# Attention and two MoE layers in one kernel: scores of two units in one TensorE visit, k and q in one load, three of sixteen quadrant copies issued by GpSimd

## The chip, the cores and the metric

The kernel runs on one core of a Trainium2 chip. The time is device microseconds from start to end of one execution. Before the change, three runs gave 1076.23, 1076.69 and 1080.57 us (median 1076.69).

## What is computed

Attention over 4 batches x 8 heads, 576 positions, head size 64, where scores under (row maximum - tau) are dropped. Its result, 2304 tokens x 512, goes through two MLP layers ("MoE" in the names) of 512 -> 2048 -> 512, the first with ELU, the second with a leaky ReLU. All is float32.

```
scores = (1/8) * q @ k^T
scores = where(scores >= max(scores) - tau, scores, -1e9)
x = softmax(scores) @ v                       # -> 2304 x 512
h = x @ w_in;   g = where(h > 0, h, exp(min(h, 0)) - 1);   x = g @ w_out
h = x @ w2_in;  g = maximum(0.01 * h, h);                  out = g @ w2_out
```

## The kernel before

**Attention.** Two heads form a pair; a *unit* is 64 query rows of a pair (128 rows on 128 partitions), 9 units for each of 16 pairs, 144 in all. A *group* is one pair with units 0 to 3 or 4 to 8, so 32 groups of 4 or 5 units (function `group`). For a group SyncE loads k, q and v (L425, L426, L428). For each unit (`unit`): four float32 matmuls of 64x64 by 64x288 make the scores s in PSUM, each in its own quarter of the array (`qk`, L445); VectorE scales them into ss in SBUF with the row minimum (L449) and makes thr from it (L454); ScalarE applies the threshold and the exponent with row sums (L457, L460) into e; VectorE takes the reciprocal of the sum (L463); GpSimd normalises e (L464); VectorE transposes e in blocks of 32x32 into the group's tile t (L472). When all units of a group are there, 16 copies of a quadrant of t into p by DMA (32 partitions each, 80 or 100 KB, L500) put the blocks in their places; then ten float32 matmuls multiply p with v (L514), and the result goes into x (L313 or L314). The first four groups go through TensorE transposes (L481) and need no copies. Buffers: two each of k, q, v, p and t, two of s in PSUM, three of ss and of e.

**MoE.** Every MoE matmul is split into three passes of float32r (a rounded high part and a rest, xh/xl, wih/wil, gh/gl). `step_h` makes h (L552), then g with gh and gl; `step_y` adds to y (L595). Seven blocks of 256 tokens of the first layer's first half (eight of sixteen slices of the hidden size) run beside the attention; all other MoE work comes after it, with 512 tokens a block. Weights are loaded as 64-bit words (wraw, L321) and turned into a high and a low part on ScalarE, VectorE and GpSimd (`weight`).

**What sets the order.** Nothing is put in order by hand. Each operation is entered with a cost, a due time vt and the engines that may do it (`op`); `Order.run` then plays the program through once at build time, and on each engine takes next, of what its plan holds to be ready, the one that is due first. The engines then run that fixed order. Constants in `KN` shift the due times and name the engines that may do a kind of work (A, D, P for ScalarE, VectorE, GpSimd); SWITCH is the planned cost when TensorE goes between float32r and float32 work.

Of the kernel before, what the change touches and what calls it, by code (L numbers as in the profile page):

```python
# [31 lines left out]
UM = 5  # L32
WT = 32 * UM
BESIDE = 7
GP = 1
AHEAD = 2
PT = ()
NA = 0
ACTI = 150
# [8 lines left out]
    pad=18, stay=455.902, late=1.3, margin=0, look=0.00334927, warm=3, tu=2231.35, lead=19463, wv0=558.362,  # L48
    wv1=105.738, early=3916.94, boff=24778.1, bdt=5036.21, yoff=2387.88, coff=7772.05, wb=1110.19, w2a=4797.07,
    o1=-2440.15, o2=2533.02, o3=4472.77, o4=-3359.29, o5=5750.16, o6=-25.7749, mo=-550.861, ka='PA', kl='AD',  # L50
    kh='PAD', ko='D', kt='D', kx='AD', kxl='DP', km='DP', kg='A', kgl='P', kgl1='D', kd='P', kc='AD', kn='P', kv='A')

# [176 lines left out]
SWITCH = 170  # L229
LAND = 2100.0  # L230
ISSUE = 400
# [25 lines left out]
def attn_moe_kernel(ctx, tc, qT, kT, vn, tau, w1i, w1o, w2i, w2o, yp, out):  # L257
# [108 lines left out]
    k_r = ring(ap_, 2, [128, 2, HALF], F32, "k")  # L366
    q_r = ring(ap_, 2, [128, 128 * UM], F32, "q")
# [4 lines left out]
    ss_r = Ring(None, 3)  # L372
    es_ = [ac.tile([128, SX], F32, name=f"e{j}") for j in range(3)]
    for t in es_:
        nc.gpsimd.memset(t[:, S:SX], 0.0)
    e_r = Ring(itertools.cycle(es_).__next__, 3)
    ident = ac.tile([128, 128], F32, name="ident")
    make_identity(nc, ident)
    sm_r = {t: ring(ap_, 4, [128, 1], F32, t) for t in ("nm", "thr", "su")}
# [5 lines left out]
    sts = [ac.tile([128, S + 2], F32, name=f"ss{j}") for j in range(3)]  # L385
# [25 lines left out]
    slots, unit_no = [], itertools.count()  # L411

    def s_of(i):
        while len(slots) <= i and len(slots) < NP * NU:
            slots.append(s_r.new())
        return slots[i] if i < len(slots) else None


    def group(gi, p, vts):
# [4 lines left out]
        k, q, v = k_r.new(), q_r.new(), v_r.new()  # L424
# [11 lines left out]
        def unit(j, vt):  # L436
            un = next(unit_no)
            s, ss, e = s_of(un), ss_r.new(), e_r.new()
            nm, thr, su = (sm_r[t].new() for t in ("nm", "thr", "su"))

            def qk():
                for h in range(2):
                    for i in range(2):
                        r = slice(64 * i, 64 * i + 64)
                        nc.tensor.matmul(s()[64 * h:64 * h + 64, i, 0:HALF], q()[r, 64 * (n * h + j):64 * (n * h + j) + 64],  # L445
                                         k()[r, h], start=True, stop=True)

            o = op((PE, mm32(HALF), qk, True), ld, [k, q, s], vt)
            o = op((DVE, dve(S) + 160, lambda: nc.vector.tensor_scalar(  # L449
                out=ss()[:, 0:S].rearrange("p (j c) -> p j c", j=2), in0=s()[:, :, 0:HALF], scalar1=scl,  # L450
                scalar2=3.0e38, op0=ALU.mult, op1=ALU.min, accum_out=nm())), [o, tau_op], [s, ss, nm], vt + KN["o1"])
            ot = op(pick(KN["kt"], P=(245, lambda: nc.gpsimd.tensor_scalar(
                             out=thr(), in0=nm(), scalar1=taup, scalar2=1.0, op0=ALU.add, op1=ALU.mult)),
                         D=(150, lambda: nc.vector.tensor_scalar(  # L454
                             out=thr(), in0=nm(), scalar1=taup, scalar2=None, op0=ALU.add))),
                [o, tau_op], [nm, thr], vt + KN["o1"])
            o = op((ACT, act(S) + 95, lambda: nc.scalar.activation(  # L457
                out=ss()[:, 0:S], in_=ss()[:, 0:S], func=AF.Prelu, bias=thr(), scale=-1.0, alpha=STEEP)),
                [ot], [ss, thr], vt + KN["o2"])
            o = op((ACT, act(S) + 190, lambda: nc.scalar.activation(  # L460
                out=e()[:, 0:S + 1], in_=ss()[:, 0:S + 1], func=AF.Exp, bias=taun, accum_out=su())),
                [o], [ss, e, su], vt + KN["o2"])
            o = op((DVE, 150, lambda: nc.vector.reciprocal(out=su(), in_=su())), [o], [su], vt + KN["o2"])  # L463
            o = op(pick(KN["kn"], P=(pool_ts(S) + 90, lambda: nc.gpsimd.tensor_scalar(  # L464
                            out=e()[:, 0:S], in0=e()[:, 0:S], scalar1=su(), scalar2=1.0, op0=ALU.mult, op1=ALU.mult)),
                        D=(dve2(S), lambda: nc.vector.tensor_scalar(
                            out=e()[:, 0:S], in0=e()[:, 0:S], scalar1=su(), scalar2=None, op0=ALU.mult), PORT)),
                   [o], [su, e], vt + KN["o3"])
            cols = slice(32 * j, 32 * j + 32)

            if not by_pe:
                turned.append(op((DVE, dve(SX) + 70, lambda: nc.vector.transpose(  # L472
                    out=blocks(tg).rearrange("p d c q -> p c d q")[:, :, :, cols],
                    in_=e().rearrange("p (c d i) -> p c d i", d=4, i=32))), [o], [e, tg], vt + KN["o3"]))
                return
            s_of(un + AHEAD)
            t = (ya if gi < GP else s_r).new()

            def tr():
                for c in range(5):  # L480
                    nc.tensor.transpose(t()[:, c // 4, c % 4 * 128:c % 4 * 128 + 128], e()[:, c * 128:(c + 1) * 128], ident)  # L481

            o = op((PE, 5 * 109, tr, True), [o], [e, t], vt + KN["o3"])
            for z, m in ((0, 4), (1, 1)):
                turned.append(op(copy_of(KN["kc"], 128 * m, lambda z=z, m=m: blocks(pg)[:, :, 4 * z:4 * z + m, cols],
                                         lambda z=z, m=m: t()[:, z, 0:128 * m].rearrange(
                                             "p (c a i) -> p a c i", c=m, a=4)), [o], [t, pg], vt + KN["o3"] + 500))

        for j in range(n):
            unit(j, vts[j])  # L490
        vt = vts[n - 1] + KN["o3"]
        got = turned
        if not by_pe:
            got = []
            for z, (a, d) in enumerate((a, d) for d in range(4) for a in range(4)):
# [6 lines left out]
                if z * NA // 16 != (z + 1) * NA // 16:  # L502
# [165 lines left out]
    TU, u, ends = KN["tu"], 0, []  # L668
# [112 lines left out]
```

## Time and profile before

| | us |
|---|---|
| median of three runs | 1076.69 |
| the profiled execution's own time | 1082.72 |
| its span, first to last instruction | 1080.7 |
| TensorE busy | 1028.9 (95%) |
| VectorE busy | 605.8 (56%) |
| ScalarE busy | 501.4 (46%) |
| GpSimd busy | 225.8 (21%) |
| mean granted clock of TensorE | 0.987 |

The profile comes from one execution. Busy time of an engine leaves out the issuing of DMAs and waits on semaphores. Shares of the whole span mix two stages: attention beside the first MoE blocks (to about 440 us), where all engines work, and MoE alone after it, where the others have little to do.

### The profile page before, as it was taken

To read this page: it belongs to the slowest core of one execution; us is meant where nothing else is said; L and a number is where in the kernel's file an instruction comes from. 1 tells how busy PE (TensorE), PEld (TensorE's weight loads), DVE (VectorE), ACT (ScalarE), POOL (GpSimd) and SP (SyncE) were. 2 spreads that over 40 slices of the span, in tenths; PEclk is the share of its full clock that TensorE was granted. 3 is DMA by queue.
4 is the path that set the end of the run, shared out by engine and by line. 5 is a ranking of instruction groups with operands and counts; after the bars stand their busy time and mean duration, and the time that the engine had idled before them with its cause. 6 is when DMAs were issued, how large, how long until landed. Compare 5 with 4: busy or idle time off the path is not lost.

```text
span 1080.7 us, 17082 instructions
## 1 busy us (share of the span) xinstructions
PE 1028.9 (95%) x6294; PEld 802.5 (74%) x6294; DVE 605.8 (56%) x1374; ACT 501.4 (46%) x1017; POOL 225.8 (21%) x317
## 2 busy tenths in 40 slices
PE   7768999999999999899999999999999999999998
PEld 3435666656766667688888889888888888888898
DVE  6887867766767675799998438961311311221221
ACT  6977867756776674354554223531222222222221
POOL 4766635444544453000000000000000000000000
PEclk9969999999999999999999999999999999999999
DMA  5678666776776677436454012420100100010010
GB/s 191 194 171 223 186 177 190 201 201 172 205 209 195 177 190 188 136 117 195 125 152 153 1 39 69 127 79 0 39 1 1 38 2 1 1 39 1 1 39 21
DMA packets 54514, 120.14 MB, mean 111 GB/s; under 512 B 10400, under 2 KB 15008, under 8 KB 54432
## 3 DMA queue, kind: packets, MB, share of 16 engines
q1 hardware_dynamic: 54432, 119.05, 38.8%
q8 instruction: 50, 0.82, 0.3%
q14 instruction: 32, 0.26, 0.1%
HBM read 67.63 MB, written 9.44 MB: 71 GB/s over the span
## 4 chain that ended last, share of the span: by engine, by line
PE 81%; SPq 6%; DMA 5%; DVE 4%; ACT 2%; issue 2%; POOL 0%; DVEq 0%; ACTq 0%
PE y L595 34%; PE h L552 20%; PE hb L552 14%; PE v L514 6%; SPq L500 6%; PE s L445 5%; DMA q<-in_qT_dram 2%; DMA p<-t 1%; DMA v<-in_vn_dram 1%; DVE ss L449 1%; ACT e L460 1%; DMA wraw<-in_w1o_dram 1%; ACT ss L457 1%; DVE g L571 1%; PE v L394 0%
## 5 line engine op out<-in xcount | busy, mean ns | idle before, releaser
L595 PE MATMUL y<-gh,woh 128*128 128x512 f32 (+1 forms) x736 | 256.0, 348 | 0.8 <-DVE ysx L314 0.8
L595 PE MATMUL y<-gl,woh 128*128 128x512 f32 (+1 forms) x736 | 252.0, 342 | 0.0
L595 PE MATMUL y<-gh,wol 128*128 128x512 f32 (+1 forms) x736 | 252.0, 342 | 0.0
L302 DVE TENSOR_TENSOR gl<-g,gh 128x512 fp32r<-128x512 f32 (+1 forms) x128 | 82.3, 643 | 269.2 <-ACT g L578 261.4
L552 PE MATMUL h<-xh,wih 128*128 128x256 f32 (+1 forms) x480 | 168.0, 350 | 14.6 <-DVE g L571 9.8
L595 PEld LDWEIGHTS y<-gh,woh 128*128 128x128 f32 x736 | 138.7, 188 | 33.1 <-issue 11.0
L552 PE MATMUL h<-xl,wih 128*128 128x256 f32 (+1 forms) x480 | 159.1, 331 | 1.3 <-POOL xl L303 1.0
L552 PE MATMUL h<-xh,wil 128*128 128x256 f32 (+1 forms) x480 | 158.3, 330 | 0.0
L595 PEld LDWEIGHTS y<-gl,woh 128*128 128x128 f32 x736 | 138.9, 189 | 16.1
L595 PEld LDWEIGHTS y<-gh,wol 128*128 128x128 f32 x736 | 138.5, 188 | 16.3
L552 PEld LDWEIGHTS h<-xh,wih 128*128 128x128 f32 x480 | 91.0, 190 | 57.3 <-issue 16.1
L449 DVE TENSOR_SCALAR_CACHE_REDUCE ss<-s,scl 128x576 f32<-128x576 f32 x144 | 116.3, 808 | 22.7 <-PE s L445 21.8
L460 ACT ACTIVATE e<-ss,taun 128x577 f32<-128x577 f32 x144 | 111.3, 773 | 32.2 <-DVE t L472 27.7
L464 POOL TENSOR_SCALAR e<-e,su 128x576 f32<-128x576 f32 x144 | 108.0, 756 | 80.6 <-DVE su L463 73.4
L472 DVE STREAM_TRANSPOSE t<-e 128x640 f32<-128x640 f32 x128 | 103.8, 831 | 32.2 <-DMA p<-t 21.7
L457 ACT ACTIVATE ss<-ss,thr 128x576 f32<-128x576 f32 x144 | 108.8, 767 | 17.0 <-DVE thr L454 16.5
L445 PE MATMUL s<-k,q 64*64 64x288 f32 x1152 | 99.6, 436 | 12.6 <-DVE ss L449 9.7
L514 PE MATMUL v<-p,v 128*64 128x320 f32 (+1 forms) x640 | 95.5, 422 | 12.8 <-DMA p<-t 7.2
L552 PEld LDWEIGHTS h<-xl,wih 128*128 128x128 f32 x480 | 91.6, 191 | 11.0 <-POOL xl L303 1.8
L552 PEld LDWEIGHTS h<-xh,wil 128*128 128x128 f32 x480 | 91.3, 190 | 8.0
L552 PE MATMUL hb<-xl,wih 128*128 128x512 f32 (+1 forms) x256 | 94.5, 369 | 0.0
L552 PE MATMUL hb<-xh,wih 128*128 128x512 f32 (+1 forms) x256 | 94.5, 369 | 0.0
(436 smaller groups left out, 1180.7 us busy)
## 6 DMA issues: line engine op xcount, KB each, us to landing
p<-t SPq DMA_DIRECT2D x256, 100.0 KB, 3.2
p<-t SPq DMA_DIRECT2D x192, 80.0 KB, 2.3
v<-in_vn_dram SPq DMA_DIRECT2D x32, 320.0 KB, 3.7
k<-in_kT_dram SPq DMA_DIRECT2D x32, 288.0 KB, 3.1
wraw<-in_w1i_dram SPq DMA_DIRECT2D x16, 512.0 KB, 3.6
wraw<-in_w1o_dram SPq DMA_DIRECT2D x16, 512.0 KB, 3.8
wraw<-in_w2i_dram SPq DMA_DIRECT2D x16, 512.0 KB, 3.5
wraw<-in_w2o_dram SPq DMA_DIRECT2D x16, 512.0 KB, 3.5
```

The source lines that it names most:

```text
L302: return pick(who, D=(dve(n), lambda: nc.vector.tensor_tensor(**args()), PORT), P=(pool_tt(n), lambda: nc.gpsimd.tensor_tensor(**args())))
L445: nc.tensor.matmul(s()[64 * h:64 * h + 64, i, 0:HALF], q()[r, 64 * (n * h + j):64 * (n * h + j) + 64], k()[r, h], start=True, stop=True)
L449: o = op((DVE, dve(S) + 160, lambda: nc.vector.tensor_scalar(out=ss()[:, 0:S].rearrange("p (j c) -> p j c", j=2), in0=s()[:, :, 0:HALF], s ...
L457: o = op((ACT, act(S) + 95, lambda: nc.scalar.activation(out=ss()[:, 0:S], in_=ss()[:, 0:S], func=AF.Prelu, bias=thr(), scale=-1.0, alpha= ...
L460: o = op((ACT, act(S) + 190, lambda: nc.scalar.activation(out=e()[:, 0:S + 1], in_=ss()[:, 0:S + 1], func=AF.Exp, bias=taun, accum_out=su())),
L464: o = op(pick(KN["kn"], P=(pool_ts(S) + 90, lambda: nc.gpsimd.tensor_scalar(out=e()[:, 0:S], in0=e()[:, 0:S], scalar1=su(), scalar2=1.0, o ...
L472: turned.append(op((DVE, dve(SX) + 70, lambda: nc.vector.transpose(out=blocks(tg).rearrange("p d c q -> p c d q")[:, :, :, cols], in_=e(). ...
L500: q.dma_start(out=to[0]()[to[1], to[2]], in_=fr[0]()[fr[1], fr[2]])
L514: nc.tensor.matmul(ps()[64 * h:64 * h + 64, 0:64 * n], v()[:, h, c, :], blocks(pg)[:, 2 * h:2 * h + 2, c], start=(c == 0), stop=(c == 4))
L552: nc.tensor.matmul(hp(), w_()[:, cs], x_()[:, 0:tb], start=(k == 0 and z == 0), stop=(k == KC - 1 and z == 2))
L571: o = op((DVE, dve(tb), lambda: nc.vector.scalar_tensor_tensor(out=g()[:, cs], in0=g()[:, cs], scalar=0.0, in1=hp(), op0=ALU.min, op1=ALU. ...
L595: nc.tensor.matmul(ysl(yg, m), w_()[:, cs], g_()[:, 0:tb], start=(first and z == 0 and share == 0), stop=(last and z == 2 and end))
```

## The change

Scores of two units are made in one TensorE operation (`units` in place of `unit`; the fifth unit of a group stays alone), with one thr and one reciprocal for both, and with four buffers of ss and e. k, q and v lie in one DRAM tensor by group; k and q come in one load of 128 partitions. The call that enters a group's copies and its value product (`values`) is made after the next group's `group`. Of the sixteen quadrant copies of a group the sixth, eleventh and sixteenth are issued by GpSimd, and the copies go round the diagonals. Costs in the planner and its constants are set anew, and with them the engines that may take some of the small operations.

```diff
-AHEAD = 2
-NA = 0
-ACTI = 150
+NG = 3
+POOLI = 1000
-SWITCH = 170
+SWITCH = 91
...
-        ld = [op(sp(128, 2304, lambda: nc.sync.dma_start(out=k(), in_=kT[hp])), [], [k], due),
-              op(sp(128, 512 * n, lambda: nc.sync.dma_start(
-                  out=q()[:, 0:128 * n], in_=qT[hp][:, 128 * u0:128 * u1])), [], [q], due)]
-        lv = op(sp(128, 2560, lambda: nc.sync.dma_start(out=v(), in_=vn[hp])), [], [v], due + 8e3)
+        kq, v = in_r.new(), v_r.new()
+        cut = 2 * HALF + 128 * n
+        ld = [op(sp(128, 4 * cut, lambda: nc.sync.dma_start(
+            out=kq()[:, 0:cut], in_=kqv[gi * NE + p][:, 0:cut])), [], [kq], due)]
+        lv = op(sp(128, 2560, lambda: nc.sync.dma_start(
+            out=v().rearrange("p h c d -> p (h c d)"), in_=kqv[gi * NE + p][:, KQV - 10 * D:KQV])), [], [v], due + 8e3)
...
-        def unit(j, vt):
-            s, ss, e = s_of(un), ss_r.new(), e_r.new()
+        def units(js, vt):
+            m = len(js)
+            s, ss, e = ([r.new() for _ in js] for r in (s_r, ss_r, e_r))
...
+                for z, j in enumerate(js):
+                    for h in range(2):
+                        for i in range(2):
...
-            o = op((PE, mm32(HALF), qk, True), ld, [k, q, s], vt)
+            oq = op((PE, m * (mm32(HALF) + 150), qk, True), ld, [kq, *s], vt)
...
+            orc = op((DVE, 150, lambda: nc.vector.reciprocal(out=su()[:, 0:m], in_=su()[:, 0:m])), oe, [su],
+                     vt + KN["o2"])
...
-        for j in range(n):
-            unit(j, vts[j])
-        vt = vts[n - 1] + KN["o3"]
+        for j in range(0, n, 2):
+            units(range(j, min(j + 2, n)), vts[j])
+        return lambda: values(gi, p, n, w, vts[n - 1] + KN["o3"], by_pe, turned, tg, pg, v, lv, blocks)
...
-            for z, (a, d) in enumerate((a, d) for d in range(4) for a in range(4)):
+            for z, (a, d) in enumerate((a, (a + r) % 4) for r in range(4) for a in range(4)):
...
-                if z * NA // 16 != (z + 1) * NA // 16:
-                    got.append(op((ACT, ACTI, lambda copy=copy: copy(nc.scalar)), turned, [pg, tg], vt + KN["o4"],
+                if z * NG // 16 != (z + 1) * NG // 16:
+                    got.append(op((POOL, POOLI, lambda copy=copy: copy(nc.gpsimd)), turned, [pg, tg], vt + KN["o4"],
                                   lat=2500))
...
-            group(gi, p, [(u + j) * TU for j in range(u1 - u0)])
+            later = group(gi, p, [(u + j) * TU for j in range(u1 - u0)])
             u += u1 - u0
+            if held is not None:
+                held()
+            held = later
+            if gi < GP or p in PT or u == NP * NU:
+                held()
+                held = None
```

Three places of the resulting order. First TensorE in the middle of the attention, before (s are score matmuls, four for a unit; h and y are MoE):

```order
L445 MATMUL s<-k,q 64x288 x4
L595 MATMUL y<-gh,woh_1310 128x256
L595 MATMUL y<-gl,woh_1310 128x256
L595 MATMUL y<-gh,wol_1321 128x256
L552 MATMUL h<-xh_2302,wih_190 128x256
L552 MATMUL h<-xl_2319,wih_190 128x256
L552 MATMUL h<-xh_2302,wil_209 128x256
L552 MATMUL h<-xh_2135,wih_340 128x256
L552 MATMUL h<-xl_2145,wih_340 128x256
L552 MATMUL h<-xh_2135,wil_360 128x256
L445 MATMUL s<-k,q 64x288 x4
```

and after, at a like place:

```order
L446 MATMUL s<-in 64x288 x8
L591 MATMUL h<-xh_2035,wih_290 128x256
L591 MATMUL h<-xl_2047,wih_290 128x256
L591 MATMUL h<-xh_2035,wil_294 128x256
L591 MATMUL h<-xh_2041,wih_290 128x256
L591 MATMUL h<-xl_2057,wih_290 128x256
L591 MATMUL h<-xh_2041,wil_294 128x256
L591 MATMUL h<-xh_2049,wih_290 128x256
L591 MATMUL h<-xl_2061,wih_290 128x256
L591 MATMUL h<-xh_2049,wil_294 128x256
L553 MATMUL v<-p,v 64x320 x10
L446 MATMUL s<-in 64x288 x8
```

Score matmuls of one unit (x4) between MoE matmuls became those of two units (x8). Counted over the whole order, TensorE's stretches of float32 work (scores, transposes, value products) between MoE matmuls are 101 before and 67 after. Of the stretches of scores alone, 55 hold one unit and 13 hold two before; 4 and 30 after.

Second SyncE over one group and the start of the next, before (p<-t are the quadrant copies):

```order
L425 DMA k<-in_kT_dram 128x576
L426 DMA q<-in_qT_dram 128x640
L500 DMA p<-t_87 32x800 x7
L428 DMA v<-in_vn_dram 128x640
L500 DMA p<-t_87 32x800 x9
```

and after:

```order
L417 DMA in<-in_kqv_dram 128x1216
L539 DMA p<-t_87 32x800 x5
L419 DMA v<-in_kqv_dram 128x640
L539 DMA p<-t_87 32x800 x8
```

Nineteen issues for a group became fifteen, thirteen of them copies.

Third GpSimd, where the other three copies stand (e is a unit's normalisation, g, gh and gl are of the MoE chain), after:

```order
L469 TENSOR_SCALAR e_91<-e_91,su 128x576
L607 TENSOR_SCALAR g<-g 128x256
L469 TENSOR_SCALAR e_92<-e_92,su 128x576
L306 TENSOR_SCALAR gh<-g 128x256
L303 TENSOR_TENSOR gl<-g,gh 128x256 x2
L539 DMA p<-t_88 32x800 x3
L469 TENSOR_SCALAR e_89<-e_89,su 128x576
L469 TENSOR_SCALAR e_90<-e_90,su 128x576
```

The three stand between the normalisation of the group's last unit and those of later units. In all there are 84 of them; before there were none.

## Rows read from the trace of the kernel before

**Rows 1.** Busy time by stage: us, busy us of each engine (instructions), granted clock, DMA share, GB/s

```profile
0.00:100.00 100.00, 74.59 (x562) 40.78 (x564) 78.44 (x213) 78.60 (x161) 62.00 (x81) 0.89 0.70 198
100.00:440.00 340.00, 318.25 (x2663) 224.18 (x2659) 229.81 (x639) 224.71 (x495) 153.17 (x225) 0.99 0.71 190
440.00:1081.00 641.00, 636.05 (x3072) 537.49 (x3072) 297.56 (x524) 198.14 (x363) 10.61 (x12) 1.00 0.18 56
```

**Rows 2.** TensorE's waits, 100 to 440 us; last row 0 to 100 us: total, times, longest

```profile
PE h L552 <- DVE g L571: 9.4, 17, 0.6
PE v L514 <- DMA p<-t: 3.4, 6, 1.4
PE s L445 <- DMA q<-in_qT_dram: 2.4, 4, 0.9
PE v L514 <- issue: 1.7, 2, 1.2
PE v L514 <- DMA k<-in_kT_dram: 1.2, 1, 1.2
...
PE v L514 <- DMA p<-t: 3.9, 2, 2.4
```

**Rows 3.** Timeline of SyncE's queue: start us, us, instruction

```profile
232.28 5.18 SPq L500 DMA_DIRECT2D p<-t  x8
237.57 0.51 SPq L428 DMA_DIRECT2D v<-in_vn_dram  x1
238.13 4.96 SPq L500 DMA_DIRECT2D p<-t  x8
243.19 0.53 SPq L425 DMA_DIRECT2D k<-in_kT_dram  x1
243.76 0.44 SPq L426 DMA_DIRECT2D q<-in_qT_dram  x1
244.30 5.29 SPq L500 DMA_DIRECT2D p<-t  x7
```

**Rows 4.** Quadrant copies on SyncE, line L500: issue in ns, first and last start

```profile
L500 SPq DMA_DIRECT2D p<-t x448: 507/589/2061, 67.4 to 434.2; - x150
```

**Rows 5.** Waits of VectorE and ScalarE, 100 to 440 us

```profile
DVE t L472 <- DMA p<-t: 19.6, 13, 3.9
...
ACT e L460 <- DVE t L472: 26.8, 17, 3.7
```

**Rows 6.** Timeline of TensorE: a visit of one unit, and one of two

```profile
118.29 1.20 PE L445 MATMUL s<-k,q 64*64 64x288 f32 x16
119.42 0.39 PE L552 MATMUL h<-xh,wih 128*128 128x256 f32 x1
...
211.02 0.28 PE L552 MATMUL h<-xl,wih 128*128 128x256 f32 x1
211.14 0.28 PE L552 MATMUL h<-xh,wil 128*128 128x256 f32 x1
211.35 0.71 PE L445 MATMUL s<-k,q 64*64 64x288 f32 x8
212.00 0.39 PE L595 MATMUL y<-gh,woh 128*128 128x256 f32 x1
212.22 0.28 PE L595 MATMUL y<-gl,woh 128*128 128x256 f32 x1
```

**Rows 7.** Line L338 of VectorE, two instructions: ns min/median/max, start

```profile
L338 DVE SCALAR_TENSOR_TENSOR wb__751<-wa__718,wb__751 x1: 650/650/650, 58.2 to 58.2; 128x512 uint32<-128x512 uint32 x1
...
L338 DVE SCALAR_TENSOR_TENSOR wb__883<-wa__847,wb__883 x1: 1155/1155/1155, 71.4 to 71.4; 128x512 uint32<-128x512 uint32 x1
```

**Rows 8.** Timelines of TensorE and VectorE: group 17's scores, last transpose, value product

```profile
225.86 1.20 PE L445 MATMUL s<-k,q 64*64 64x288 f32 x16
...
238.52 0.84 DVE L472 STREAM_TRANSPOSE t<-e 128x640 f32<-128x640 f32 x1
...
258.74 1.08 PE L514 MATMUL v<-p,v 128*64 128x256 f32 x8
```

More of the change, by code (lines that the diff above doesn't have):

```diff
@@ L384, in attn_moe_kernel @@
     scl = ac.tile([128, 1], F32, name="scl")
[L385 removed]
+    sts = [ac.tile([128, S + 2], F32, name=f"ss{j}") for j in range(4)]
     ss_r.make = itertools.cycle(sts).__next__
@@ L457, in unit @@
[L457 to L463, printed above, removed]
@@ L476, in unit @@
[L476 to L487, printed above, removed]
@@ L489, in group @@
-        for j in range(n):
-            unit(j, vts[j])
-        vt = vts[n - 1] + KN["o3"]
+                             out=thr()[:, 0:m], in0=nm()[:, 0:m], scalar1=taup, scalar2=None, op0=ALU.add))),
+                [*om, tau_op], [nm, thr], vt + KN["o1"])
+            oe = []
+            for z in range(m):
+                o = op((ACT, act(S) + 95, lambda z=z: nc.scalar.activation(
+                    out=ss[z]()[:, 0:S], in_=ss[z]()[:, 0:S], func=AF.Prelu, bias=thr()[:, z:z + 1], scale=-1.0,
+                    alpha=STEEP)), [ot], [ss[z], thr], vt + KN["o2"])
+                oe.append(op((ACT, act(S) + 190, lambda z=z: nc.scalar.activation(
+                    out=e[z]()[:, 0:S + 1], in_=ss[z]()[:, 0:S + 1], func=AF.Exp, bias=taun,
+                    accum_out=su()[:, z:z + 1])), [o], [ss[z], e[z], su], vt + KN["o2"]))
@@ new lines, in copies, with turn @@
+            def copies(src, t, ot, c0, c1, z):
+                cols = slice(32 * js[z], 32 * js[z] + 32)
+                nn = 128 * (c1 - c0)
+                turned.append(op(copy_of(KN["kc"], nn, lambda: blocks(pg)[:, :, c0:c1, cols],
+                                         lambda: src().rearrange("p (c a i) -> p a c i", a=4, i=32)),
+                                 [ot], [t, pg], vt + KN["o3"] + 500))
+            def turn(dst, c, z):
+                nc.tensor.transpose(dst, e[z]()[:, c * 128:(c + 1) * 128], ident)
@@ new lines, in units, with tr @@
+            if not by_pe:
+                for z, j in enumerate(js):
+                    cols = slice(32 * j, 32 * j + 32)
+                    turned.append(op((DVE, dve(SX) + 70, lambda z=z, cols=cols: nc.vector.transpose(
+                        out=blocks(tg).rearrange("p d c q -> p c d q")[:, :, :, cols],
+                        in_=e[z]().rearrange("p (c d i) -> p c d i", d=4, i=32))), [on[z]], [e[z], tg], vt + KN["o3"]))
+            elif gi < GP:
+                for z in range(m):
+                    t = ya.new()
+                    def tr(t=t, z=z):
+                        for c in range(5):
+                            turn(t()[:, c // 4, c % 4 * 128:c % 4 * 128 + 128], c, z)
+                    o = op((PE, 5 * 109, tr, True), [on[z]], [e[z], t], vt + KN["o3"])
+                    copies(lambda t=t: t()[:, 0], t, o, 0, 4, z)
+                    copies(lambda t=t: t()[:, 1, 0:128], t, o, 4, 5, z)
+            else:
+                for z in range(m):
+                    t = v_ps.new()
+                    def tr(t=t, z=z):
+                        for c in range(4):
+                            turn(t()[:, c * 128:c * 128 + 128], c, z)
+                    o = op((PE, 4 * 109, tr, True), [on[z]], [e[z], t], vt + KN["o3"])
+                    copies(lambda t=t: t(), t, o, 0, 4, z)
+                t = v_ps.new()
+                def tr(t=t):
+                    for z in range(m):
+                        turn(t()[:, z * 128:z * 128 + 128], 4, z)
+                o = op((PE, m * 109, tr, True), on, [*e, t], vt + KN["o3"])
+                cols = slice(32 * js[0], 32 * js[0] + 32 * m)
+                turned.append(op(copy_of(KN["kc"], 128 * m, lambda: blocks(pg)[:, :, 4, cols].rearrange("p a (z i) -> p a z i", i=32),
+                                         lambda t=t: t()[:, 0:128 * m].rearrange("p (z a i) -> p a z i", a=4, i=32)),
+                                 [o], [t, pg], vt + KN["o3"] + 500))
```

99 lines of the change are left out of this document (48 added, 51 removed).

## The prediction

> **What bounds the kernel now.** I read the busy time by stage first [rows 1]. From 440 us on TensorE is busy for 636.05 of 641 us: that stage can give back at most 5 us, whatever is done. From 100 to 440 us, where attention runs beside the first MoE blocks, it is busy for 318.25 of 340 us, so 21.75 us are idle; in the first 100 us 25.4 us are idle. All that the change touches lies ahead of 440 us, and what it saves there moves the rest of the program forward, since TensorE is the engine that the last stage waits for.
>
> Second, TensorE's waits [rows 2]: from 100 to 440 us it waits 9.4 us for VectorE's g of the MoE chain, 3.4 us for quadrant copies (p<-t) ahead of a value product, 1.7 us for "issue" there, 2.4 and 1.2 us for loads of q and k. In the first 100 us another 3.9 us go to quadrant copies. No single wait is long; the question is whether one thing lies behind them.
>
> Third, SyncE's queue [rows 3]. One cycle from the copies at 232.28 to those at 244.30 is 12.0 us, and each issue begins about 0.1 us after the end of the one before: 16 copies, one v, one k, one q, and nothing idle. In all, 448 copies go out from 67.4 to 434.2 us [rows 4], 28 groups at 13.1 us. The 16 DMA engines are busy for 71% of that stage [rows 1], so it is issuing, not moving, that fills the cycle. SyncE's queue paces the groups, and TensorE with 94% busy runs just beside it. The queue's lateness shows elsewhere: VectorE's transposes wait 19.6 us in 13 places for copies to free the t buffer, and ScalarE waits 26.8 us for those transposes [rows 5]. VectorE's lateness is what TensorE sees as "g".
>
> Fourth, what a visit costs [rows 6]. MoE matmuls start 0.12 us apart. A visit of one unit takes 211.14 to 212.22 = 1.08 us between MoE starts where two spacings alone would be 0.24, so 0.84 us. Two units in one visit take 119.42 - 118.29 = 1.13 us against 212.00 - 211.35 = 0.65 us for one, so the second unit adds 0.48. Two apart cost 1.68 us, two together 1.32: **0.36 us are the visit's own**.
>
> **The change part by part.**
>
> *Two units in a visit.* By the order of the instructions TensorE goes from MoE matmuls to attention 101 times before and 67 times after (before, the planner already put some units together). 34 x 0.36 = **12.2 us** less on TensorE's own path. Nothing hides this: the engine is 94% busy there. The pair needs both score buffers free at once, but its first matmul waits only for the first of them, so I add no wait. VectorE's thr and reciprocal are made once for two units; VectorE is busy 229.81 of 340 us [rows 1], so I count that as nothing beyond what follows.
>
> *k and q in one load, three copies on GpSimd.* On SyncE a group falls from 16 to 13 copies, and from three loads to two. With (5.18 + 4.96)/16 = 0.63 us for a copy and 0.5 for a load [rows 3], 12.0 becomes 12.0 - 1.9 - 0.5 = 9.6 us: the queue is then idle for a fifth of the time and no longer paces. What is late next is TensorE itself. I take back the waits that this queue made: copies 3.4 + 1.7 + 3.9 = 9.0, loads 2.4 + 1.2 = 3.6, and of the 9.4 for g one half, 4.7, since half of the wait on VectorE may be its own work [rows 2]. Together **17.3 us**. Bounds: nothing, if the waits form again in another place, and the whole 21.75 + 3.9 us.
>
> *GpSimd's issues.* 84 copies go to its queue, behind the group's last normalisation, and the next units' normalisations and gl stand behind them. The trace of before has no issue by GpSimd. The nearest row is SyncE's copy, 0.507 to 2.061 us [rows 4]. GpSimd is busy 153.17 of 340 us [rows 1], 45% or 5.9 us of a group's 13.1. Three issues of 0.51 to 2.06 us make it 7.4 to 12.1 us; I take the short end, since the same kind of transfer is nearest, and add **2 us** for gl that comes later. Bounds: nothing, and the case "GpSimd paces" below.
>
> One instruction of VectorE with two inputs from SBUF (L338) took 650 ns at 58.2 us and 1155 ns at 71.4 us [rows 7], so something can hold it; the rows do not say what. The Trainium skill (SBUF — State Buffer, "Who interferes with whom" and "SBUF: two separate sides") says that the two share a pair of ports under an exclusive lock, and that a DMA issued by GpSimd starves while VectorE holds it, a 620 ns transfer taking some 3100 ns. That speaks against this change; the rows fit a conflict of the two, but no run here shows it for a DMA. By the same page a VectorE instruction with one SBUF input outside its two-port modes does not take the lock. If it held for each issue the group would stand at 5.9 + 3 x 3.1 = 15.2 us on GpSimd (an estimate from that page), and the program 28 x 2.1 = 59 us longer than now; by the row's price the sum keeps its 2 us.
>
> *"Values a group later".* The order of TensorE does not show this. Counted over the 23 groups from the eighth to the thirtieth, a group's value product stands behind 10.3 later units of scores before, and behind 8.2 after: **nearer**, by about two units, not farther. Deferring the call only changes the order in which the planner hears of it. So slack for the copies shrinks; this is the first rival.
>
> *Planner's numbers, the new layout, four buffers for e and ss.* They move work between ScalarE, VectorE and GpSimd (GpSimd takes weights' low words and some gh, VectorE some xl). All of these have idle time (VectorE 68%, ScalarE 66%, GpSimd 45% busy in the middle stage [rows 1]). I cost them at nothing; without that cover each microsecond would count fully. Behind 440 us TensorE is full, so nothing there either.
>
> Sum: -12.2 - 17.3 + 2 = **-27.5 us**. Against the profiled execution: span 1080.7 to 1053.2, its own time 1082.72 to 1055.2. The median of the runs lies 6.0 us below that time, 1076.69, so I predict 1076.7 - 27.5 = **1049 us**.
>
> **The rivals.**
>
> *Values wait again.* Group 17 as an example [rows 8, 3]: its last scores end at 227.0, its last transpose at 239.4, its copies start at 244.3, the product at 258.7: 31.7 us. Of these, 10.3 units at 13.1/4.5 us are 30.0. After the change a group takes 13.1 - 27.5/28 = 12.1 us, so 8.2 units are 22.0, and with the same 1.7 us of rest 23.7 us stand ahead of the product. Needed are 12.4 to the transpose, 14.4 - 3 x 0.63 = 12.5 from the first copy to the product, and one more unit's pass because two go together (VectorE's transpose 0.84 and, much the same, its read of the scores), 26.6 us. The forecast holds if the 12.4 shrink by 2.9, about what one wait on VectorE and one on ScalarE take (1.5 us and 1.6 us a time [rows 5]) and what SyncE no longer causes. If they shrink by half of that, a group takes 12.1 x 25.1/23.7 = 12.8 us, 28 x 0.3 = 8 us less than now, and with the first stage's 3.9 us 12 are won: **1065 us**. If by nothing, 13.6 us, and the program would stand at 1087. For it: the count of the order. Against it: SyncE is no longer the queue that holds the buffers.
>
> *GpSimd paces: slower.* Its group is 5.9 + 3c for an issue of c; beyond c = (13.1 - 5.9)/3 = 2.4 us it exceeds today's 13.1 us a group. An issue as long as the longest on SyncE, 2.06, that half the time waits out an L338 of 1.155 is 2.64 us: 13.8 us, +0.7 x 28 groups = +20, **1097 us**. For it: normalisations and gl have no other engine. Against it: L338 turns weights, in the first stage and after 440 us, and most copies go out between.
>
> *Everything goes.* If no wait of the middle stage is left (21.75), with the copies of the first stage (3.9) and the visits (12.2), it is -38 us: **1039 us**. For it: the queue lies behind most of them. Against it: g's chain has three engines of its own.
>
> *It does nothing*, because TensorE's clock or a new wait takes the visits' gain: 1077.
>
> **How the numbers follow.** Forecast 0.55, everything goes 0.14, values wait 0.19, GpSimd paces 0.09, nothing 0.03. The range 1033 to 1072 holds the first two and most of the third, and leaves out the slower case, "nothing" and the tails. A measurement of this kernel tells about 0.5%, 5.4 us, from no change: below 1071.3 is faster, above 1082.1 slower. Faster is 0.55 + 0.14 + 0.12 of "values wait" = 0.81; same is 0.05 more of that case and "nothing", 0.08; slower its last 0.02 and GpSimd's 0.09, 0.11.
>
> **What would show it.** Right: value products that start without idle time, SyncE's queue with gaps between groups, transposes' wait on copies nearly gone, the last quadrant copy near 407 us in place of 434.2 [rows 4], one group every 12.1 us. Right for the visits: s matmuls in runs of two units, MoE to attention 67 times. Wrong: p<-t ahead of the value products at 1 us or more in most groups (values wait), GpSimd over 90% busy from 100 to 410 us or normalisations that wait behind DMA issues (GpSimd paces), or a granted clock well below 0.97 in the middle stage.

## The result and the profile after

The changed kernel takes **1066.64 us** (median of four runs, 1065.84 to 1070.21) where the kernel before took 1076.46 beside it: a ratio of 0.9895, 95% interval 0.9873 to 0.9917, so 11.3 us faster by the ratio (9.8 by the two medians), less than half of the 27.5 forecast. One execution of a run below (a_fill) took 2567 us and is left out of its ratio. The profiled execution has a span of 1068.4 us (own time 1070.21), 12.3 less than before.

Busy time by stage (us; TensorE, its weight loads, VectorE, ScalarE, GpSimd; granted clock, DMA share, GB/s), to be held against [rows 1]:

```profile
0.00:100.00 100.00, 77.10 (x558) 43.42 (x559) 77.95 (x184) 77.73 (x162) 50.57 (x69) 0.81 0.60 187
100.00:440.00 340.00, 317.42 (x2713) 235.31 (x2712) 244.16 (x575) 227.06 (x497) 194.82 (x315) 0.98 0.73 198
440.00:1069.00 629.00, 624.81 (x3027) 529.00 (x3026) 273.96 (x470) 203.39 (x371) 19.03 (x28) 1.00 0.17 54
```

TensorE's idle time from 100 to 440 us is 22.6 us, as good as the 21.75 of before. Its waits there, to be held against [rows 2]:

```profile
PE h L591 <- ACT g L603: 4.2, 9, 0.5
PE s L446 <- DMA in<-in_kqv_dram: 4.2, 3, 2.0
PE v L553 <- DMA p<-t: 3.8, 3, 3.2
PE h L591 <- DVE g L610: 3.7, 6, 0.9
PE s L446 <- DVE ss L450: 2.7, 1, 2.7
```

The wait on VectorE's g fell from 9.4 to 3.7, but one on ScalarE's g, one for the load `in` and one for ss stand in its place; copies ahead of a value product are 3.8, in three places, where they were 3.4.

The quadrant copies (issue in ns min/median/max, first and last start), against [rows 4]; then waits of VectorE and ScalarE, against [rows 5]; then waits of SyncE's queue from 100 to 430 us:

```profile
L539 SPq DMA_DIRECT2D p<-t x364: 507/590/2264, 69.2 to 420.2; - x182
...
L539 POOL DMA_DIRECT2D p<-t x84: 496/498/685, 69.4 to 413.5; - x84
```

```profile
DVE t L489 <- DMA p<-t: 6.1, 6, 3.4
...
ACT e L464 <- DVE t L489: 0.4, 2, 0.2
```

```profile
SPq L419 <- PE v L553: 24.1, 11, 4.3
SPq L539 <- DVE t L489: 15.5, 13, 4.4
```

So the signs that were named for SyncE's queue came: it has gaps (it now waits for TensorE to free v and for transposes), transposes wait 6.1 us for copies where it was 19.6, ScalarE 0.4 for transposes where it was 26.8. The last copy starts at 420.2, 14 us earlier, where 27 were forecast.

Where the 12.3 us of the two profiled executions came from, by the starts of value products: the eighth at 127.6 before and 132.1 after, the last (32nd) at 435.4 and 423.6. The start lost 4.5, the 24 groups between took 291.6 in place of 307.7 (12.15 us a group in place of 12.82), and what follows was the same within 0.6. Up to the start of the last product TensorE has done the same 3202 matmuls in both (before, then after; its busy time is the second figure):

```profile
0.00:435.35 435.35, 389.24 (x3202) 263.26 (x3203) 307.04 (x849) 302.69 (x653) 215.17 (x305) 0.97 0.71 192
0.00:423.64 423.64, 380.24 (x3202) 268.59 (x3202) 310.16 (x738) 297.98 (x645) 243.81 (x381) 0.94 0.71 197
```

So of the 11.7 us by which the last product starts earlier, 9.0 are shorter work on TensorE and 2.7 less idle time: 6.4 less between the eighth product and the last (20.1 to 13.7), 3.7 more ahead of the eighth (26.0 to 29.7).

Per group, mean of the 28 groups with copies, worked out from the trace, from the start of the group's last score matmul on (us; below zero, the product starts before the last copy lands; the last row is the period of the 24 groups):

| | before | after | all 16 copies by SyncE | six by GpSimd | eight |
|---|---|---|---|---|---|
| last scores to last transpose | 13.4 | 11.6 | 12.0 | 11.6 | 11.8 |
| to the first copy | 4.7 | 0.3 | 1.4 | 0.1 | 0.2 |
| first to last copy | 11.2 | 9.4 | 10.9 | 7.3 | 7.9 |
| landing of the last | 2.6 | 2.5 | 2.3 | 3.4 | 3.9 |
| to the value product | 0.1 | 0.5 | -0.2 | 1.1 | 0.8 |
| **scores to product** | **32.1** | **24.4** | **26.4** | **23.5** | **24.6** |
| period of a group | 12.82 | 12.15 | 13.32 | 11.84 | 12.50 |

The three right-hand columns are runs below, with the changed kernel's order held. In the order a product stands 8.2 units behind its scores, 4.5 units make a group, so scores to product is 8.2/4.5 of the period and some 1.7 us: 23.8 by the period of 12.15. The order ties the chain and the period to each other, so the table alone does not tell which drives which.

### The profile page after: what moved, and what is told of

Read it like the earlier page. It is cut to its first block, busy times and chain, and to the rows that moved or that the text cites. A ratio compares the mean times of both kernels' runs of the same rounds, so it can differ in the third digit from the quotient of the medians.

```text
span 1068.4 us, 17123 instructions
## 1 busy us (share of the span) xinstructions
PE 1019.3 (95%) x6294; PEld 807.7 (76%) x6294; DVE 596.1 (56%) x1228; ACT 508.2 (48%) x1027; POOL 264.4 (25%) x411
## 4 chain that ended last, share of the span: by engine, by line
PE 81%; DMA 6%; SPq 4%; DVE 3%; ACT 2%; issue 2%; POOL 0%; POOLq 0%; ACTq 0%; DVEq 0%
PE y L634 35%; PE h L591 20%; PE hb L591 15%; PE v L553 7%; PE s L446 5%; SPq L539 3%; DMA p<-t 2%; DMA in<-in_kqv_dram 2%; DMA wraw<-in_w1o_dram 1%; DVE t L489 1%; DVE ss L450 1%; PE y L484 1%; DMA wraw<-in_w1i_dram 0%; ACT e L464 0%; ACT p L313 0%
## 5 line engine op out<-in xcount | busy, mean ns | idle before, releaser
L591 PE MATMUL h<-xh,wih 128*128 128x256 f32 (+1 forms) x480 | 163.7, 341 | 15.8 <-ACT g L603 7.2
L591 PEld LDWEIGHTS h<-xh,wih 128*128 128x128 f32 x480 | 90.9, 189 | 43.6 <-issue 10.4
L469 POOL TENSOR_SCALAR e<-e,su 128x576 f32<-128x576 f32 x144 | 110.2, 776 | 40.5 <-DVE su L467 35.3
L461 ACT ACTIVATE ss<-ss,thr 128x576 f32<-128x576 f32 x144 | 105.3, 769 | 16.8 <-DVE thr L456 16.4
L446 PE MATMUL s<-in 64*64 64x288 f32 x1152 | 95.5, 443 | 11.3 <-DVE ss L450 7.0
L553 PE MATMUL v<-p,v 128*64 128x320 f32 (+1 forms) x640 | 98.0, 439 | 7.3 <-DMA p<-t 4.3
```

Of the source, the lines that this page charges most:

```text
L446: nc.tensor.matmul(s[z]()[64 * h:64 * h + 64, i, 0:HALF], q()[r, at:at + 64], k()[r, h], start=True, stop=True)
L461: o = op((ACT, act(S) + 95, lambda z=z: nc.scalar.activation(out=ss[z]()[:, 0:S], in_=ss[z]()[:, 0:S], func=AF.Prelu, bias=thr()[:, z:z + ...
L469: on = [op(pick(KN["kn"], P=(pool_ts(S) + 90, lambda z=z: nc.gpsimd.tensor_scalar(out=e[z]()[:, 0:S], in0=e[z]()[:, 0:S], scalar1=su()[:, ...
L553: nc.tensor.matmul(ps()[64 * h:64 * h + 64, 0:64 * n], v()[:, h, c, :], blocks(pg)[:, 2 * h:2 * h + 2, c], start=(c == 0), stop=(c == 4))
L591: nc.tensor.matmul(hp(), w_()[:, cs], x_()[:, 0:tb], start=(k == 0 and z == 0), stop=(k == KC - 1 and z == 2))
```

## The experiments

Each run has its own kernel before beside it, with medians of 1077.35 to 1078.34, so the ratios are compared. A difference to the change is the difference of the two ratios times 1077 us; the interval behind it joins the two intervals as the root of their squares. "Order held" means that every engine's other instructions stand as they stood; "planned anew" means that the planner made another order.

**1. The three copies alone, and undone** (order held).

```diff
 b_gp_copies: the kernel before
-  copy(nc.sync)
+  copy(nc.gpsimd if z in (5, 10, 15) else nc.sync)
 a_sp_copies: the changed kernel
-  op((POOL, POOLI, lambda copy=copy: copy(nc.gpsimd)), ...
+  op((POOL, POOLI, lambda copy=copy: copy(nc.sync)), ...
```

> The kernel before, its order of instructions unchanged on TensorE, VectorE and ScalarE; only the sixth, eleventh and sixteenth quadrant copy of each group are issued by GpSimd in place of SyncE. If SyncE's queue made the waits (the forecast's step): copies, loads and half of g are won, 9.0 + 3.6 + 4.7 = 17 us, less 2 for GpSimd: about 1061 us. If it did not pace the kernel: 1076 us, within 3. If GpSimd's issues hurt: above 1080 us.

Measured: 1074.68 us, ratio 0.9971 [0.9951, 0.9992], 3.1 us.

> The changed kernel with its order unchanged on TensorE, VectorE and ScalarE; all sixteen copies are issued by SyncE. If the value products are just in time (they start 0.3 us after the last landing in the median), each group's copies land up to 3 x 0.63 = 1.9 us later and the products wait: 10 to 45 us slower, 1077 to 1110 us. If there is slack behind the copies: 1067 us, within 3. If GpSimd's three issues are a burden, it is faster than 1064 us.

Measured: 1098.08 us, ratio 1.0183 [1.0149, 1.0217]: 31 us (±4) over the change.

TensorE's waits from 100 to 440 us, first of the kernel before with three copies by GpSimd:

```profile
PE h L553 <- DVE g L572: 9.8, 18, 0.6
PE v L515 <- issue: 3.6, 6, 0.9
```

and of the changed kernel with all copies by SyncE:

```profile
PE v L553 <- DMA p<-t: 21.6, 14, 3.9
PE s L446 <- DMA in<-in_kqv_dram: 6.4, 7, 1.7
```

In the first the waits for loads are gone, but the wait for g stands as it stood in [rows 2]: so it was not SyncE's. In the second 14 products wait for copies, and part of the wait lies inside them: they start up to 0.6 us before the last copy lands, and from the eighth to the last they keep TensorE busy for 80.6 us in place of 69.5 in the changed kernel (a lower granted clock is a part of that; L553 alone, the changed kernel first):

```profile
132.08:423.64 291.56, 69.48 (x480) 40.65 (x480) 0.99 0.75 201
133.19:452.88 319.69, 80.55 (x481) 43.39 (x481) 0.98 0.69 184
```

One edit is worth 3 us in one order and 31 in the other. The chain that ended last, its shares of the span by line, shows it within each run; before, after, and the run with all copies by SyncE (SPq is SyncE's queue):

```profile
by line: PE y L595 34.2%; PE h L552 19.9%; PE hb L552 14.4%; PE v L514 6.1%; SPq L500 5.7%; PE s L445 5.1%; issue 1.8%; DMA q<-in_qT_dram 1.6%; DMA p<-t 1.3%; DMA v<-in_vn_dram 1.0%; DVE ss L449 0.8%; ACT e L460 0.8%; DMA wraw<-in_w1o_dram 
```

```profile
by line: PE y L634 34.7%; PE h L591 19.8%; PE hb L591 14.6%; PE v L553 6.8%; PE s L446 4.6%; SPq L539 3.5%; DMA p<-t 2.4%; issue 1.6%; DMA in<-in_kqv_dram 1.6%; DMA wraw<-in_w1o_dram 1.2%; DVE t L489 0.9%; DVE ss L450 0.5%; PE y L484 0.5%; 
```

```profile
by line: PE y L634 30.7%; PE h L591 17.0%; PE hb L591 14.2%; SPq L539 11.9%; PE v L553 6.2%; DMA p<-t 2.8%; PE s L446 2.5%; issue 2.0%; DMA in<-in_kqv_dram 1.8%; DMA wraw<-in_w1o_dram 1.1%; DVE ss L450 0.8%; DVE t L489 0.8%; SPq L419 0.7%; 
```

SyncE's copies hold 5.7% of the span before (62 us) and still 3.5% after (37 us): the queue has gaps, and yet its issues lie on the path.

**2. More and fewer of SyncE's issues** (the changed kernel, order held).

```diff
 a_two_loads: k and q in two issues
-  dma_start(out=kq()[:, 0:cut], in_=kqv[...][:, 0:cut])
+  [dma_start(out=kq()[:, a:z], in_=kqv[...][:, a:z]) for a, z in ((0, 2 * HALF), (2 * HALF, cut))]
 a_gp6 (a_gp8: 1, 3, 7, 9, 13)
-  copy(nc.sync)
+  copy(nc.gpsimd if z in (2, 7, 12) else nc.sync)
```

> The changed kernel, every other instruction in its order, with the load of k and q issued as two again (28 more issues by SyncE). Nothing is left out of the computation. The prediction gave 3.6 us to loads' waits and 0.5 us of SyncE per group to this: by it 1070 and TensorE's waits for in 3 us longer. Theory 'SyncE no longer paces anything' (it now waits 45 us for TensorE to free v and 15 us for transposes): within 1 us of the change, 1065.5 to 1067.5.

Measured: 1071.32 us, ratio 0.9938 [0.9915, 0.9962]: 4.6 us (±3.5) over the change.

> The changed kernel, every other instruction in its order, with six of a group's 16 quadrant copies issued by GpSimd in place of three. Nothing is left out of the computation. Theory 'the value products are just in time, so an earlier last copy is time won': the last landing comes 3 x 0.6 = 1.8 us earlier, p<-t waits (3.8 us) go, 1062 to 1065. Rival 'GpSimd, which also normalises, is late then': three issues more are 1.6 us a group behind which normalisations stand, y and t wait on e, 1069 to 1080.

Measured: 1057.87 us, ratio 0.9808 [0.9775, 0.9840]: 9.4 us (±4.2) **under** the change, the fastest of these runs.

> The changed kernel with eight of a group's 16 copies by GpSimd, every other instruction in its order. Nothing is left out of the computation. Theory 'the chain paces': from scores to product 24.4 us with three, 23.5 with six; two more take SyncE's stretch from 7.3 to 6.1 us, if GpSimd's eight (8 x 0.55 = 4.4 us) are not later: 1053 to 1058. Rival 'GpSimd's normalisations are now late': 1060 to 1075, t waits for e at over 10 us in all.

Measured: 1073.34 us, ratio 0.9958 [0.9935, 0.9981]: 6.8 us (±3.4) over the change.

TensorE's longest waits of the three, in this order, 100 to 440 us:

```profile
PE v L554 <- DMA p<-t: 7.1, 7, 3.2
```

```profile
PE h L592 <- ACT g L604: 4.3, 9, 0.5
PE h L592 <- DVE g L611: 3.6, 6, 0.9
PE v L554 <- DMA p<-t: 2.3, 3, 1.1
```

```profile
PE v L554 <- issue: 7.8, 5, 1.9
PE h L592 <- DVE g L611: 5.0, 7, 1.2
```

One issue more on SyncE delays the copies behind it, and the products wait 7.1 us for them; the load itself is not waited for. Three fewer bring the last copy 2.1 us nearer to the first, and SyncE's copies fall to 1.2% of the chain:

```profile
by line: PE y L635 36.6%; PE h L592 21.0%; PE hb L592 14.8%; PE v L554 7.4%; PE s L446 5.2%; DMA p<-t 1.9%; SPq L539 1.2%; issue 1.1%; DMA wraw<-in_w1i_dram 1.0%; ACT e L464 0.9%; PE y L484 0.6%; DVE t L489 0.5%; DMA wraw<-in_w1o_dram 0.5%;
```

With eight the copies come apart on GpSimd, which is argued from its timeline alone: the sign named for late normalisations, transposes that wait for e for over 10 us, came (13.6 us from 100 to 420), but with six it was 12.6. The timeline (start us, us, instruction) shows a group's copies with other work between them:

```profile
239.00 0.74 POOL L303 TENSOR_TENSOR gl<-g,gh 128x256 fp32r<-128x256 f32 x1
239.70 0.41 POOL L306 TENSOR_SCALAR gh<-g 128x256 fp32r<-128x256 f32 x1
240.06 0.55 POOL L539 DMA_DIRECT2D p<-t  x1
240.65 1.47 POOL L469 TENSOR_SCALAR e<-e,su 128x576 f32<-128x576 f32 x2
242.07 0.55 POOL L539 DMA_DIRECT2D p<-t  x1
242.65 0.75 POOL L303 TENSOR_TENSOR gl<-g,gh 128x256 fp32r<-128x256 f32 x1
243.32 0.51 POOL L539 DMA_DIRECT2D p<-t  x1
```

From the table: against the change the chain is +2.0 us with none, -0.9 with six, +0.2 with eight. If the period follows the chain by 4.5/8.2, 28 groups make +31, -14 and +3 us of it; measured are +31, -9.4 and +6.8: about the size with none and with six, twice as much with eight. Only the issuing engine of copies was changed in these runs, and the time went with it, so SyncE's issues are shown to set a part of the period. By which way is not shown: the loads stand in the same queue, and with six by GpSimd TensorE's wait for `in` (4.2 us) is gone, while that for copies fell by 1.5.

**3. What a visit is worth** (order held): the second unit's scores stand behind the next MoE step, 109 visits for 67.

```diff
-  for z, j in enumerate(js): (scores of unit z)
+  flush(); qk1(0); behind.append(lambda: qk1(1))
 step_h, step_y, behind their matmuls:
+  flush()
```

> The changed kernel in its own order, but the second unit's score matmuls stand behind the MoE matmuls that followed the pair, so TensorE goes to attention 109 times in place of 67. If a visit costs 0.36 us of TensorE's path: 42 x 0.36 = 15 us slower, 1082 us. If the engine's waits take it up: 1067 us, within 4.

Measured: 1071.93 us, ratio 0.9948 [0.9929, 0.9966]: 5.7 us (±3.1) over the change, 0.136 us a visit. From the eighth product to the last TensorE's idle time fell from 13.7 to 11.2 us: visits filled a part of what had been waiting.

> The changed kernel with six copies of a group by GpSimd (that alone: 1057.9 us) and the second unit of each pair scored behind the next MoE step, so 109 visits in place of 67, every other instruction in its order. Nothing is left out of the computation. Theory 'the chain from a group's scores to its value product paces the changed kernel, and hides part of what visits cost': 42 visits cost 5.7 us where three copies go by GpSimd (0.135 us each); with the chain 2 us shorter TensorE is nearer to being the bound and they cost more, 0.25 to 0.36 us each, 1068 to 1073. Rival 'a visit is worth 0.135 us whatever waits': 1062 to 1065.

Measured: 1068.16 us, ratio 0.9915 [0.9889, 0.9941]: 11.5 us (±4.5) over the run with six copies, 0.27 us a visit, for the same 42. Where the chain is shorter a visit costs about twice as much, though the two intervals overlap, and that of the second (7 to 16 us) holds the 15 us that 42 visits of 0.36 would make. TensorE's idle time is 10.4 us without the visits and 10.1 with them there: hardly any of their work fell into waits.

**4. TensorE's clock in the start** (order held). The granted clock is 0.81 in the first 100 us after, 0.89 before [rows 1]. Fillers go into idle times:

```diff
+  matmul(bank()[:, 0:128], ident, ident)    # 9 and 8 times (a_fill_early), and 10 and 14 (a_fill)
```

> The changed kernel, every instruction in its order, with 41 small float32 matmuls of the identity put into four of TensorE's idle times in the start (9 ahead of the third pair's scores, 8 ahead of the first value product, 10 and 14 ahead of the MoE steps that wait for g at 71.2 and 79.6 us); they write a score-free bank that the next value product overwrites. Nothing is left out of the computation. Theory 'the change gave time back through TensorE's clock in the start' (in the profiled run 20.6 us of clock lost ahead of the eighth product against 11.9 before; over single executions a lost us is about half a us of span): the drops at 12 and 70 us go or shrink, lost clock of the whole run falls from 19 to about 10, and the time falls by 3 to 6 us, 1061 to 1064. Rival 'the granted clock is only a sign of idle time and costs nothing of its own': the time stays at 1066 to 1068, or rises by what the fillers overshoot.

Measured: 1068.29 us, ratio 0.9902 [0.9868, 0.9936]: 0.8 us (±4.4) over the change.

> As the run with 41 fillers, with the first two places alone (17 fillers, at 9.4 and 23.8 us). Nothing is left out of the computation. Theory 'clock': the drop at 12.3 us (10.2 us long at half) goes, 5 us of lost clock less, 2 to 3 us of time, 1063.5 to 1065. Rival: 1066 to 1068.

Measured: 1065.62 us, ratio 0.9889 [0.9849, 0.9928]: 0.6 us (±4.9) under.

Busy time by stretch, 0 to 30 and 60 to 90 us, of the changed kernel and then with 41 fillers:

```profile
0.00:30.00 30.00, 22.09 (x128) 10.47 (x129) 20.00 (x53) 19.66 (x40) 13.29 (x23) 0.77 0.59 202
60.00:90.00 30.00, 22.10 (x143) 11.18 (x136) 27.04 (x56) 23.86 (x49) 16.56 (x22) 0.66 0.60 172
```

```profile
0.00:30.00 30.00, 24.21 (x184) 13.69 (x185) 21.36 (x57) 21.48 (x43) 13.53 (x24) 0.94 0.60 204
60.00:90.00 30.00, 24.70 (x196) 17.11 (x197) 27.66 (x55) 24.33 (x50) 17.55 (x22) 0.87 0.62 179
```

The clock came back, 0.987 to 0.992 over the executions against 0.977 to 0.986, some 7 us of lost clock, and the time did not follow. My theory that the change gave time back through the clock, 3 to 6 us, was not borne out: a gain beyond some 4 us is excluded, a smaller one is not.

**5. Orders planned anew.** Parts in other combinations, each with its own order:

```diff
 a_weights:       wv0=558.362, wv1=105.738, early=3916.94 in KN, as before
 a_start_single:  units one at a time in the first four groups
 a_later:         the value product waits for the third later group's first scores
 b_pairs:         the changed code, NG=0, with the planner's numbers of before (b_pairs_gp: and three copies by GpSimd)
 b_numbers:       the code of before with the planner's numbers of the change
 a_no_gp:         NG=0
 a_single:        units one at a time throughout
 a_nudge4:        margin=20
```

> The changed kernel with the first weights' due times of before (wv0, wv1, early); the planner sets the order anew. The first 130 us lose 20.6 us of full clock against 11.9 before, and the first seven groups end 4.5 us later than before. If the early weights in VectorE's queue cause it: 5 to 8 us faster, 1059 to 1062 us, with the granted clock of the first 130 us back at 0.91. If the start is slow for another reason: 1067 us, within 3.

Measured: 1081.48 us, ratio 1.0034 [1.0014, 1.0053].

> The changed kernel with units one at a time in the first four groups (those that TensorE transposes); 72 visits in place of 67. If pairs make the start uneven and so lose the clock: 5 us faster, 1061 us, first value products of group 7 before 130 us. If not: 5 visits x 0.36 = 2 us slower, 1068 us.

Measured: 1070.34 us, ratio 0.9933 [0.9907, 0.9959]. Its eighth product starts 4.8 us earlier, which the rest more than gives back.

> The changed kernel where a group's value product may start only behind the first scores of the third group after it: 10.9 later units of scores in place of 8.2, 72 visits in place of 67; the planner sets the order anew. If the nearer value products are where the waits formed again: p<-t ahead of the products gone (3.8 us from 100 to 430 us), 5 visits x 0.36 = 2 us paid, and the loads' waits with them: 1062 to 1066 us. If they are not the cause: 1068 us or above.

Measured: 1082.87 us, ratio 1.0045 [1.0027, 1.0063]. Products no longer wait (1.3 us), but 42 MoE matmuls fewer are done beside attention and the stage behind the last product takes 653.3 us in place of 644.8. That the products are just in time was not mended by putting them later.

> The kernel before with its own planner's numbers and all copies on SyncE, but units in pairs and k and q in one load: 73 visits in place of 101, value products behind 10.1 later units as before. If the visits are the whole gain: 28 x 0.36 = 10 us faster than before, 1066 to 1068 us, as fast as the changed kernel. If pairs need the other parts of the change: 1073 us or above.

Measured: 1076.83 us, ratio 0.9987 [0.9971, 1.0002].

> As b_pairs with its order unchanged, but three copies of a group issued by GpSimd. The same edit in the kernel before was worth 3 us. If the two parts add: 3 us under b_pairs, about 1063 us, faster than the changed kernel. If the pair leaves SyncE's queue the slack anyway: the same as b_pairs within 2 us.

Measured: 1076.87 us, ratio 0.9985 [0.9965, 1.0006].

> The kernel before with only the planner's numbers of the change (its lead and offsets, which engine takes which step, the costs of a switch, an issue and a copy); units one at a time, three loads a group, all 16 copies by SyncE. 89 visits, a value product 8.8 later units behind its scores. Nothing is left out of the computation. Theory 'the numbers carry the rest': the parts alone gave -3.1 and -1.4 us, the whole -10.5, so the numbers alone give -5 to -8, 1070 to 1073. Theory 'the numbers only fit the other parts': with all copies on SyncE and the value products 1.5 units nearer they are late as in the run with the copies put back, p<-t ahead of the value products over 8 us, and the time is 1080 to 1095. The prediction, which cost the numbers at nothing: 1077 within 3.

Measured: 1089.86 us, ratio 1.0095 [1.0072, 1.0117]: a miss for the theory that the numbers carry the rest and for the prediction. The theory that they only fit the other parts had it: the products wait 5.8 us for copies from 100 to 440 us and 2.6 before.

> The changed kernel planned anew with all 16 copies on SyncE: pairs, one load for k and q, the change's numbers. 69 visits, 8.5 later units. Nothing is left out of the computation. Theory 'an order with near value products needs GpSimd's copies': 1080 to 1095, p<-t over 10 us in all; the run with the order held was 1098, the order planned for it wins a part back. Theory 'a planned order makes up for the copies' (as the pairs with before's numbers were the same with and without GpSimd's copies): 1066 to 1072.

Measured: 1082.28 us, ratio 1.0041 [1.0024, 1.0057].

> The changed kernel planned anew with units one at a time throughout (one load for k and q, three copies by GpSimd and the numbers stay). 75 visits, 8.0 later units. Nothing is left out of the computation. Theory 'a visit costs 0.36 us on the path': 8 visits more plus the second thr and reciprocal, 1070 to 1073. Theory 'a visit costs 0.135 on the path, the order decides': 1066 to 1070 if the plan is as good, and TensorE's start stretch is 4 us shorter, as in the run with the first four groups single.

Measured: 1086.52 us, ratio 1.0068 [1.0049, 1.0087], against every expectation: 63 MoE matmuls fewer beside attention, 655.7 us behind the last product, and 34.1 us idle ahead of the eighth in place of 29.7.

> The changed kernel with one number of the planner moved (margin 0 to 20), so that it makes another order of the same kind: 69 visits, 8.0 later units, all parts of the change in. Nothing is left out of the computation. Theory 'what the change won beyond its parts lies in this one order': 1070 to 1080, like the other orders planned anew. Theory 'it lies in the kind of order (pairs, GpSimd's copies, near value products)': 1065 to 1069.

Measured: 1072.73 us, ratio 0.9954 [0.9935, 0.9973]: another order of the same kind, 6.4 us (±3.1) slower.

Two things follow. Alone, the parts give little: the pairs with one load 1.4 us and both together 1.6, neither clear of no change, the copies 3.1, the numbers minus 10. Undone from the whole one at a time they give 4.6 (load), 5.7 (visits, 109 of them where the kernel before had 101) and 31 (copies). They aren't terms of a sum. And a_nudge4, which differs in nothing but the order, is 6.4 us slower; the other variants of the change planned anew are 4 to 19 slower, with part and order mixed. So this group says little on any one part; only the runs with the order held do. The copies' way round the diagonals and the later call of `values` have no run of their own.

## Why the prediction was right in its sign and wrong in its size

- **The step that failed is "the queue is then idle for a fifth of the time and no longer paces. What is late next is TensorE itself", and with it the 17.3 us of waits taken back.** The queue's idle time was forecast rightly; that it then paces nothing was not. TensorE's idle time to the last product is 43.4 us where it was 46.1: 2.7 won, not 17.3. The wait for g, 4.7 of the sum, wasn't SyncE's (9.8 with the queue relieved). In place of the waits taken back stand others (g on two engines 7.9 us, loads 4.2, copies 3.8, ss 2.7 from 100 to 440 us), and SyncE's issues go on pacing, as in the rival "values wait again": products stand 8.2 units behind their scores, 13 copies at 0.63 us stand one behind another between the two, and three more copies or three fewer on SyncE make the whole program 31 us slower or 9 faster. That rival's own sign, 1 us or more ahead of most products, did not come in the changed kernel (three waits from 100 to 440 us), only with all copies by SyncE (14). A queue with gaps can still pace when what it issues is a chain that someone waits for at the end. Why the waits for g, ss and the start stayed or grew is open.
- **"Nothing idle" in the queue before held for the one cycle that was read**, 12.0 us, not for the groups, which took 12.82. So the named sign "one group every 12.1 us" came (12.15), and yet a group gained only 0.67 us of the 1.0 forecast, since 13.1, taken over all 28 groups, is too high for these 24.
- **The rival "values wait again" gave 1065 us, and 1066.64 came, by luck in the number.** It wanted the 12.4 us to the last transpose to shrink by 1.45 of the 2.9 needed; the mean over groups fell from 13.4 to 11.6, 1.8. The count of units in the order was right, and deserved the larger chance. But its period was too long (12.8, measured 12.15), and its sum was 8 us won in the groups and 3.9 in the first stage, where 16 were won in the 24 groups and 4.5 lost in the start.
- **Visits: 0.36 us fits on the engine, and is too much on the path of the changed kernel.** TensorE's busy time to the last product fell by 9.0 us, of the size of the 12.2 forecast, though the granted clock fell as well. "Nothing hides this: the engine is 94% busy there" failed: put back, the same work costs 0.136 us a visit in the changed kernel, and 0.27 with a shorter chain, where 0.36 isn't excluded. At 0.136, 34 visits are 4.6 us, not 12.2.
- **One load for k and q** was sized well: 3.6 forecast for loads, 4.6 (±3.5) measured, but through the copies behind it.
- **GpSimd's issues:** taken at SyncE's short end, 0.51 us; 0.50 measured. By the rule of the Trainium skill (SBUF — State Buffer, "Who interferes with whom" and "SBUF: two separate sides"), which the prediction weighed at 3.1 us an issue, an estimate, the program would have been 59 us slower; the longest of 84 issues took 0.685 us, and of 224 in the run with eight 0.691. No run here sets a VectorE instruction of that kind beside an issue on purpose.
- **Planner's numbers "cost nothing"** can't be kept as a step: with the code of before they cost 10 us, and with pairs, one load and GpSimd's copies the numbers of before (b_pairs_gp) give 1076.87 us where those of the change give 1066.64, the order being another too.
- The clock, a named sign of failure, stayed at 0.98 in the middle stage.

## What to carry to other kernels

Before taking back the waits behind a queue, follow one item from its first producer to its last consumer and compare that latency with the slack that the order gives it; if the change takes slack as well, the latency can set the period, and gaps in a queue or 94% busy on an engine do not speak against it. Measure parts with the order held: where a planner makes the order, another order alone cost 6.4 us, more than most of the parts. And try the dose: three copies moved gave a part, six gave 9 us more, eight took it back, probably because the second queue does other work between.

## What the runs showed of the hardware that I had not expected

- A copy's issue is cheaper on GpSimd than on SyncE (medians 498 against 590 ns), while its landing takes longer: 3.7 to 3.8 us from issue against 3.1 to 3.3 on SyncE's queue in the same execution. That is no property of the queue alone: with six copies by GpSimd the two are alike (3.7 to 3.9 and 3.5 to 4.1), and with all by SyncE a landing takes 2.4 to 2.6.
- The Trainium skill (DMA: Bandwidth & Descriptors, "Issuing engines are not separate DMA queues") says that issuing from several engines saves only the time to initiate a DMA, usually small beside the transfer. For one copy the trace agrees: 0.59 us to issue, 3.1 to 3.3 to land. For a group it is the reverse: 13 issues one behind another take 9.4 us and the landing of the last 2.5, and issuing three more of them from GpSimd won 9.4 us.
- Some 7 us of TensorE's lost clock in the start, given back, changed the time by less than the 4 us that could be seen: the fillers' rows show the clock regained and the time unmoved. What ends the start in its place was not tried. And a granted clock of 0.95 need not mean slower work: the profile of a_two_loads shows it from 137 us to the end, and what follows the last product took the same 644.8 us as in the changed kernel.
